# A fused attention and SwiGLU block on one core: the last of the seven products of two output phases is split into seven once more, with its operand sums on VectorE

## The chip, the core and the metric

The kernel runs on one core of a Trainium2 chip. The metric is the device time of one execution in microseconds (us), as the median of several runs. TensorE (PE) does the matrix products and writes to PSUM, which has eight banks of 128x512 fp32. VectorE (DVE) and ScalarE (ACT) read PSUM and the on-chip SBUF, GpSimd (POOL) does a few small operations, and DMA transfers are issued from the queues of SyncE (SP), ACT and POOL. Each engine works through its own instructions in order and waits on semaphores for the others.

## The reference

A transformer block over 2048 rows of width 1024, modulated by a conditioning vector `c`:

```python
mod = (silu(c) @ w_mod).reshape(1, 6, 1, -1)          # sa, ca, ga, sb, cb, gb
h = layernorm(x) * (1 + ca) + sa
q = (h @ wq) as 32 heads of 128                       # keys, values: the last 512 rows of each cache, 4 heads
o = softmax(q k^T * 128**-0.5) v
x = x + ga * (o @ wo)                                 # wo: 4096 x 1024
h = layernorm(x) * (1 + cb) + sb
out = x + gb * ((silu(h @ w_gate) * (h @ w_up)) @ w_down)   # w_gate, w_up: 1024 x 3584, w_down: 3584 x 1024
```

All inputs are bfloat16, and the output is bfloat16.

## The kernel before

The rows are worked in two halves (`sc` 0 and 1) of 1024 rows, first through attention, each half followed by its output phase (`o_phase(sc)`, the product with `wo`), and then through the feed-forward part, each half a run of `gate_up` steps followed by its down phase (the product with `w_down`, called with `f_out` and `f_hook`). In time the order is: attention and output phase of half 0, of half 1, then gate/up and down of half 0, of half 1.

Most large products are not multiplied block by block. A product of 2x2 blocks is written as seven block products in place of eight, of sums and differences of the blocks (the Strassen-Winograd form). For the two output products `seven_products` (L1030) does this. Its left operand is held in four blocks `X[0]` to `X[3]`, each `nk` slices of 128x512 (`nk` is 16 for `wo`, 14 for `w_down`); its right operands are the weights, of which four combined versions were formed earlier by VectorE and written to DRAM (`wo_sum`, `wd_sum`). The products run in the order `ORDER = (1, 2, 6, 5, 3, 7, 4)`, which the text counts as steps 0 to 6. A step has four parts, `j` = 0 to 3, one for each 128 rows, and one part is `nk` matmuls of 128x128 by 128x512 into one bank. PSUM banks hold running totals from one step to the next: `AB[j]` and `BB_[j]` are the two sets of four.

Between the steps VectorE makes the sums of the left operand in place (L1041), ScalarE copies a bank to SBUF (`snap`, L832), and VectorE finishes an output tile in `residual` (L1107) with up to three operations: add of bank and copy (L1117), product with the gate row (L1118), add of `x_res` (L1119). In step 6 one product per part is the whole sum for an output tile, so `residual` takes two operations there, L1112 and L1119. A `hook(idx, j)` after each part runs other work beside the phase: weight loads of a coming step on the ACT queue (`load`), the layer normalisation of the next rows (`ln_pair`, whose modulations are L443), the four sums of the next left operand (`h_sums`, L838 to L850, 128x2048 each), and the sums of the coming gate and up weights (`w_sums` by `ws`, L901).

The order on each engine is the order in which the program emits it; a tracker (`T.op`) adds the semaphore waits that the buffers demand. After an output or down phase comes `gate_up(q, None)` (L1552), which begins with product 1 of the gate weights into bank `ga`, product 2 into `gb_`, a copy of `gb_` on ScalarE, and VectorE's sum `g_sum` (L830) of `ga` and the copy. Then products 1 and 2 of the up weights follow into `ua` and `ub`, a copy and `u_sum` (L830), and then product 6 into `ga` again and later into `ua` again. So product 6 waits until `g_sum` has read `ga`, and until `u_sum` has read `ua`. The gate/up weights come by `take_w(q)` on the SP queue, into three slots in turn.

Memory is one arena with fixed offsets; where two tiles share a place, the later one waits for the users of the earlier.

Of the kernel before, what the change touches and what calls it, by code (L numbers as in the profile page):

```python
# [4 lines left out]
AF = mybir.ActivationFunctionType  # L5
BF16 = mybir.dt.bfloat16
F16 = mybir.dt.float16
# [124 lines left out]
def bass_adaLN_cond__sliding_block_cached__swiglu_ffn__prompt_kernel(  # L132
# [126 lines left out]
    with nc.Block() as block:  # L259

        @block.gpsimd
        def _(g):
# [764 lines left out]

            ORDER = (1, 2, 6, 5, 3, 7, 4)

            def seven_products(nk, X, XBf, offs, s1, ver, AB, BB_, out, sj, own_s1, hook, early=(0,) * 4, halves=False):  # L1030
# [48 lines left out]
                for j in range(TPC):  # L1079
                    prod(3, j, BB_[j], True)  # L1080
                    snap(*sj[j], BB_[j])
                    inplace(3, j, 2, [(jc(X[2], j), jc(X[3], j), jc(X[0], j), [S[2][j]] + XBf[3])])
                    hook(3, j)
                for j in range(TPC):
                    prod(4, j, BB_[j], False)
                    out(0, j, 1, AB[j], BB_[j], None)
                    hook(4, j)
                for j in range(TPC):
                    prod(5, j, AB[j], False)
                    out(1, j, 1, AB[j], None, sj[j])  # L1090
                    hook(5, j)
                for j in range(TPC):
                    if halves and j == TPC - 1:
                        lo, hi = slice(0, CH // 2), slice(CH // 2, CH)
                        T.op(ACT, lambda: A.activation(sj[j][0][:, lo], bank(AB[j])[:, lo], AF.Copy), writes=[PB[AB[j]], sj[j][1]])
                        prod(6, j, BB_[j], True, c=lo)
                        out(1, j, 0, BB_[j], None, sj[j], lo)
                        prod(6, j, AB[j], False, c=hi)
                        out(1, j, 0, AB[j], None, None, hi)
                    else:  # L1100
                        prod(6, j, AB[j], False)
                        out(1, j, 0, AB[j], None, None)
                    hook(6, j)
                for n, blk in ((2, 0), (4, 1), (3, 2)):
                    arena.regs.append((offs[blk], offs[blk] + nk * KB, S[n]))

            def residual(t, c0, row, a_bk, b_bk, sj, ring, dst, db, c=slice(0, CH)):  # L1107
                tm, tb = ring
                tm = tm[:, c]
                rw = rowb[row][:, c0:c0 + CH][:, c]  # L1110
                if b_bk is None and sj is None:
                    T.op(DVE, lambda: V.tensor_tensor(tm, bank(a_bk)[:, c], rw, MULT), reads=[B_row[row]], writes=[PB[a_bk], tb])  # L1112
                else:
                    if b_bk is not None:
                        snap(tm, tb, b_bk)
                        sj = (tm, tb)
                    T.op(DVE, lambda: V.tensor_tensor(tm, bank(a_bk)[:, c], sj[0][:, c], ADD), reads=[sj[1]], writes=[PB[a_bk], tb])  # L1117
# [19 lines left out]
            def loader(sc, raw, sums, nk, kind, places):  # L1137
                pair = raw.rearrange("(p h q) n -> h q p n", h=2, q=P)
                src = {1: pair[0][:, :, 0:CH], 2: pair[1][:, :, 0:CH], 3: pair[1][:, :, CH:D]}
                for n, i in ((5, 1), (6, 2), (4, 3), (7, 0)):  # L1140
                    src[n] = sums[:, :, i, :].rearrange("p q n -> q p n")
                got = {}

                def load(idx, which=None):
                    n = ORDER[idx]
                    dt = BF16 if n < 4 else F16
                    k0 = 0
                    got.setdefault(idx, [])
                    for q, (off, m) in enumerate(places[idx]):
                        if which is not None and q not in which:  # L1150
                            k0 += m
                            continue
                        b_ = _Buf("%sv%d_%d_%d" % (kind, sc, idx, q))
                        ap = arena.at(off, [m, CH], dt, [b_])
                        T.op(Q_ver[q][idx % 3], lambda: A.dma_start(ap, src[n][:, k0:k0 + m, :]),
                             reads=[B_uw[(kind, p)] for p in range(k0, k0 + m)] if n > 3 else [], writes=[b_])
                        got[idx] += [(ap[:, k, :], b_) for k in range(m)]
                        k0 += m

                return load, lambda idx, k: got[idx][k]  # L1160

            def attention(sc, lo, pre, tick):
                hi = (sc + 1) * NI
# [170 lines left out]
            attend(0, 1, pre0, tick0)  # L1334

            def o_out(sc, sj, rings):
                def out(tt, j, half, a_bk, b_bk, s):
                    t = (2 * sc + tt) * TPC + j
                    ring = rings(tt, j, half)
                    residual(t, half * CH, 0, a_bk, b_bk, s, ring, x_res[:, t, half * CH:(half + 1) * CH], B_x[t])  # L1340
                return out

            def o_phase(sc, hook):
# [208 lines left out]
            def gate_up(q, pq, fill=None):  # L1552
# [16 lines left out]
                    snap(*sn[1], xb)  # L1569
                if a:  # L1570
                    g_sum(q, 0, ga, sn[0])
                    if q % FP == 1:
                        ws(2)
                if b:
# [50 lines left out]
                        ws(2)  # L1625

            def f_out(sc):
                def out(tt, j, half, a_bk, b_bk, s, c=slice(0, CH)):
# [4 lines left out]
                    residual(t, c0, 1, a_bk, b_bk, s, tms[i % 2], y_b[:, i, c], B_y[i], c)  # L1633
                    T.op((Q_out + Q_fin)[i], lambda: SP.dma_start(of[t * P:(t + 1) * P, c0:c0 + CH][:, c], y_b[:, i, c]), reads=[B_y[i]])
                return out

            for sc in range(2):
# [7 lines left out]
                for r in range(FP + 1):  # L1645
# [70 lines left out]
```

The softmax here doesn't subtract the row's maximum and nothing guards it: scores larger than these inputs give would overflow.

## Time and profile before

| | |
|---|---|
| median of 4 runs | 1152.6 us (1151.49 to 1152.9) |
| the profiled execution's own time | 1152.76 us |
| its span, first to last instruction | 1151.0 us |
| PE busy | 1143.5 us, 99% of the span |
| DVE busy | 822.5 us, 71% |
| ACT busy | 525.9 us, 46% |
| granted TensorE clock | 1.0 |
| step 6 of the output phase of half 1 | 625.91 to 639.72 us |
| step 6 of the down phase of half 0 | 881.55 to 893.63 us |

How the profile is read: a group row gives line, engine, operation, the tiles it writes and reads, shapes and count, then busy time, the mean duration of one in ns, and the idle time of the engine just before them with what ended it. A timeline row gives start, duration, engine, line and operation, and in square brackets the idle time before it and what ended that. A row by windows gives, for a stretch, its length, the busy time of each engine with the number of instructions touched, the granted clock and the DMA share. Matmuls are pipelined: a 128x512 matmul is shown with some 379 ns from start to end, while the next starts 216 ns after it.

### The profile page before, as it was taken

What the parts mean: (1) busy time and instruction counts of PE and PEld (TensorE: products, weight loads), DVE (VectorE), ACT (ScalarE), POOL (GpSimd) and SP (SyncE); (2) the same over time, 40 slices, a digit from 0 to 9 for tenths busy, and PEclk for the clock granted to TensorE, in tenths of its full rate; (3) what the DMA queues carried; (4) which work ended last, traced back from release to release, by engine and by line L of the source; (5) the groups of instructions that cost most, each with busy time, mean ns of one, the idle gap of its engine ahead of it and who ended that gap; (6) DMA issues with size and microseconds to landing.
All of it is one profiled execution on the core that took longest, in us unless ns stands there. A gap on an engine that the chain in (4) does not pass through costs nothing.

```text
span 1151.0 us, 18014 instructions
## 1 busy us (share of the span) xinstructions
PE 1143.5 (99%) x6991; PEld 584.4 (51%) x6991; DVE 822.5 (71%) x1644; ACT 525.9 (46%) x719; POOL 50.2 (4%) x107
## 2 busy tenths in 40 slices
PE   8999999999999999999999999999999999999999
PEld 5566565554446666566444444444444444444444
DVE  5768779857667777776757789877658777776536
ACT  4757777721127777777010354544110445444110
POOL 1100102100000000001000000000000000000000
DMA  9889999988617998946864423323783433233343
GB/s 317 148 186 225 226 214 218 216 204 202 201 41 179 205 213 188 211 105 156 192 199 128 111 73 87 97 74 106 209 224 121 119 87 97 74 106 131 129 156 110
DMA packets 300373, 180.83 MB, mean 157 GB/s; under 512 B 140928, under 2 KB 289152, under 8 KB 300288
## 3 DMA queue, kind: packets, MB, share of 16 engines
q1 hardware_dynamic: 241632, 108.90, 42.2%
q10 hardware_dynamic: 54336, 55.05, 15.1%
q0 software_dynamic: 4320, 15.73, 4.6%
q8 instruction: 55, 0.90, 0.4%
q14 instruction: 30, 0.25, 0.1%
HBM read 126.75 MB, written 19.93 MB: 127 GB/s over the span
## 4 chain that ended last, share of the span: by engine, by line
PE 97%; DMA 1%; DVE 1%; SPq 0%; ACT 0%; issue 0%; POOLq 0%; DVEq 0%
PE ps L269 97%; DMA arena<-in_A_wq_dram 1%; DMA arena<-in_A_wo_dram 1%; DVE arena L830 0%; ACT arena L800 0%; SPq L337 0%; SPq L306 0%; DVE arena L847 0%; DVE arena L951 0%; DVE arena L901 0%; PE ps L273 0%; DVE st L424 0%; DVE arena L822 0%; DVE tmp L1112 0%; DVE arena L1119 0%
## 5 line engine op out<-in xcount | busy, mean ns | idle before, releaser
L269 PE MATMUL ps<-arena 128*128 128x512 f16 (+2 forms) x6778 | 1138.6, 331 | 4.6 <-POOL arena L416 2.0
L269 PEld LDWEIGHTS ps<-arena 128*128 128x128 bf16 (+1 forms) x6778 | 577.2, 98 | 559.5 <-DVE arena L830 5.8
L800 ACT ACTIVATE arena<-ps 128x1024 bf16<-128x1024 f32 x256 | 261.7, 1022 | 47.0 <-PE ps L269 35.3
L833 ACT ACTIVATE tmp<-ps 128x512 f32<-128x512 f32 x167 | 99.7, 597 | 293.0 <-PE ps L269 282.2
L901 DVE TENSOR_TENSOR arena<-arena 128x512 f16<-128x512 bf16 x328 | 133.5, 420 | 3.0
L830 DVE TENSOR_TENSOR arena<-ps,tmp 128x512 bf16<-128x512 f32 (+1 forms) x134 | 91.9, 686 | 52.1 <-PE ps L269 34.7
L833 ACT ACTIVATE nsc<-ps 128x512 f32<-128x512 f32 x84 | 50.1, 597 | 93.3 <-PE ps L269 90.9
L822 DVE TENSOR_TENSOR arena<-ps,rl 128x512 f16<-128x512 f32 x128 | 88.5, 691 | 4.9 <-DVE rl L819 0.5
L830 DVE TENSOR_TENSOR arena<-ps,nsc 128x512 f16<-128x512 f32 x84 | 57.3, 687 | 40.3 <-PE ps L269 30.0
L819 DVE RECIPROCAL rl<-ps 128x4 f32<-128x4 f32 x128 | 23.2, 181 | 74.6 <-PE ps L269 73.5
L1117 DVE TENSOR_TENSOR tmp<-ps,tmp 128x512 f32<-128x512 f32 x32 | 22.1, 690 | 63.4 <-ACT tmp L833 60.8
L1532 ACT ACTIVATE arena<-arena 128x512 f16<-128x512 f16 x84 | 49.8, 624 | 32.8 <-DVE arena L830 32.8
L1041 DVE TENSOR_TENSOR arena<-arena 128x2048 f16<-128x2048 f16 (+3 forms) x56 | 55.6, 1012 | 9.8 <-PE ps L269 9.2
L833 ACT ACTIVATE arena<-ps 128x512 f32<-128x512 f32 x16 | 9.6, 597 | 91.8 <-PE ps L269 91.8
L951 DVE TENSOR_TENSOR arena<-arena 128x512 f16<-128x512 bf16 x120 | 47.9, 420 | 2.2 <-DMA arena<-in_A_wo_dram 1.2
L424 DVE BATCH_NORM_STATS2 st<-x_res 128x6 f32<-128x512 bf16 x58 | 39.6, 682 | 3.6 <-DMA x_res<-in_A_x_dram 3.4
L602 DVE SCALAR_TENSOR_TENSOR arena<-arena 128x1024 bf16<-128x1024 bf16 x32 | 38.9, 1217 | 0.0
L1547 DVE TENSOR_TENSOR arena<-arena 128x512 f16<-128x512 f16 x84 | 35.0, 417 | 0.3
L1118 DVE TENSOR_TENSOR tmp<-tmp,rowb 128x512 f32<-128x512 f32 (+1 forms) x49 | 33.6, 686 | 1.8
L438 DVE TENSOR_SCALAR nsc<-x_res,mv,rstd 128x1024 f16<-128x1024 bf16 (+1 forms) x30 | 16.2, 539 | 13.5 <-DMA arena<-nsc 13.5
L1119 DVE TENSOR_TENSOR arena<-tmp,x_res 128x512 bf16<-128x512 f32 (+1 forms) x33 | 22.3, 676 | 1.1
L830 DVE TENSOR_TENSOR arena<-ps,rowb 128x512 f16<-128x512 f32 x28 | 19.3, 689 | 3.8 <-ACT rowb L833 3.3
(80 smaller groups left out, 295.0 us busy)
## 6 DMA issues: line engine op xcount, KB each, us to landing
arena<-in_A_wq_dram SPq DMA_DIRECT2D x30, 512.0 KB, 5.2
arena<-wo_sum ACTq DMA_DIRECT2D x7, 2048.0 KB, 8.6
arena<-in_B_w_gate_dram SPq DMA_DIRECT2D x28, 512.0 KB, 3.8
arena<-in_B_w_up_dram SPq DMA_DIRECT2D x28, 512.0 KB, 5.1
arena<-wd_sum ACTq DMA_DIRECT2D x8, 1792.0 KB, 8.1
arena<-in_B_w_down_dram ACTq DMA_DIRECT2D x6, 1792.0 KB, 7.2
arena<-in_A_wo_dram POOLq DMA_DIRECT2D x16, 512.0 KB, 5.9
wo_sum<-arena SPq DMA_DIRECT2D x16, 512.0 KB, 4.5
```

The lines of the kernel that those rows point to most:

```text
L269: T.op(PE, lambda: TE.matmul(out_ap, lhsT, rhs, start=start, stop=stop, skip_group_check=skip), reads=reads, writes=[bank_buf])
L424: T.op(DVE, lambda: V.bn_stats(st_[sl][:, hf * 6:hf * 6 + 6], x_res[:, t, hf * 512:hf * 512 + 512]), reads=[B_x[t]], writes=[B_st[sl]])
L602: T.op(DVE, lambda: V.scalar_tensor_tensor(mt[n % 2], mt[n % 2], 1.0, sc_row, op0=ALU.mult, op1=ALU.mult, accum_out=mcol[:, n:n + 1]), rea ...
L800: T.op(ACT, lambda: A.activation(ex_s[es][:, 2 * kp:2 * kp + 2, :], banks2(SCB + 2 * kp), AF.Exp, scale=att_scale), writes=[PB[SCB + 2 * k ...
L822: T.op(DVE, lambda: V.tensor_tensor(o_s[os_].rearrange("p (a b) d -> p a b d", a=2), psap(PVB * 512, [[512, 2], [130, 2], [1, P]]), rlb, A ...
L830: T.op(DVE, lambda: V.tensor_tensor(out, bank(ba), other, ADD), reads=[ob2], writes=[PB[ba], ob])
L833: T.op(ACT, lambda: A.activation(dst, bank(bk), AF.Copy), writes=[PB[bk], db])
L901: T.op(st, lambda: eng.tensor_tensor(o, a, b, op), reads=rd, writes=[wr])
L951: T.op(DVE, lambda: V.tensor_tensor(o, a, b, SUB), reads=rd, writes=[wr])
L1041: T.op(DVE, lambda: V.tensor_tensor(o, a, b, SUB), reads=rd, writes=[sb])
L1532: T.op(ACT, lambda: A.activation(o, s_, AF.Silu), reads=[sb], writes=[ob])
L1547: T.op(DVE, lambda: V.tensor_tensor(gu[blk][:, p, :], o, s_, MULT), reads=[sb, ob], writes=[B_gu[blk][p]])
```

## The change

Step 6 of two of the four phases, `o_phase(1)` and the down phase of half 0, is no longer four parts of `nk` matmuls 128x512. A class `_Deep` splits this one product again into seven products of halves: `h = nk / 2` slices by `Q = 256` columns, for two groups `g` of rows. `left` makes four sums of the left block `X[3]` after step 3 into the place of the no longer used `X[0]`; `right` makes four sums of the weights of step 6, two within step 5 and two after the first two small products, one of them in place. `run` orders the fourteen small products, and `keep` (ScalarE, 128x256) and `plus` (VectorE, 128x256) carry partial sums from bank to SBUF. The output tiles of this step then need the three operations of `residual` and not two. The second and third of the very last tile are put in `late_out` and emitted inside the next `gate_up`, after its `g_sum`; in the down phase its store goes with them.

Other work changes place in these two phases: `h_sums` goes from step 6 to step 4 (in the down phase its first two operations to the end of step 3), the modulations of `ln_pair` are drained ahead of it, `w_sums` of the down phase goes from step 6 to step 0, the weights of step 6 of the down phase are loaded after part 1 of step 4 (not part 3) into another place and in three transfers, the weights of step 5 in `o_phase(1)` have another place, and the tiles of `o_phase(1)` use `sj[j]` as scratch.

```diff
+late_out = []
...
+class _Deep:
...
+    def left(self, off, free):
+        h, x, Q = self.h, self.x, CH // 2
+        self.b_s = [_Buf("dS%d" % n) for n in range(4)]
+        s = self.s = arena.at(off, [4, h, Q], F16, self.b_s)
+        for b_ in self.b_s:
+            for f in free:
+                b_.absorb(f)
+        a11, a12, a21, a22 = x[:, 0:h, 0:Q], x[:, h:, 0:Q], x[:, 0:h, Q:], x[:, h:, Q:]
+        for (n, a, b, op, rd) in ((0, a21, a22, ADD, []), (1, s[:, 0], a11, SUB, [0]), (3, a12, s[:, 1], SUB, [1]), (2, a11, a21, SUB, [])):
+            T.op(DVE, lambda: V.tensor_tensor(s[:, n], a, b, op), reads=self.xb + [self.b_s[m] for m in rd], writes=[self.b_s[n]])
+            yield
+    def right(self, off, free):
+        h, Q = self.h, CH // 2
+        self.b_t = [_Buf("dT%d" % n) for n in range(3)]
+        self.b_5 = [_Buf("d5%d" % n) for n in range(2)]
+        t = self.t = arena.at(off, [3, h, Q], F16, self.b_t)
+        self.p5 = arena.at(off + 3 * h * Q * 2, [2, Q], F32, self.b_5)
+        for b_ in self.b_t + self.b_5:
+            for f in free:
+                b_.absorb(f)
...
+        for step in (0, 1, 3, 2):
+            for (m0, m1, ((lo, lb, lof), (hi, hb, hof))) in self.segs:
+                o = [t[:, n, m0:m1, :] for n in range(3)]
+                b11, b12, b21, b22 = lo[:, :, 0:Q], lo[:, :, Q:], hi[:, :, 0:Q], hi[:, :, Q:]
+                if step == 3:
+                    b3 = _Buf("dT3")
+                    b3.absorb(lb)
+                    arena.regs.append((lof, lof + (m1 - m0) * KB, [b3]))
+                    self.b_3.append(b3)
+                    T.op(DVE, lambda: V.tensor_tensor(b12, b22, b12, SUB), reads=[hb, lb], writes=[b3])
+                else:
+                    a, b, rd = ((b12, b11, [lb]), (b22, o[0], [hb, self.b_t[0]]), (b21, o[1], [hb, self.b_t[1]]))[step]
+                    T.op(DVE, lambda: V.tensor_tensor(o[step], a, b, SUB), reads=rd, writes=[self.b_t[step]])
+            yield
...
+    def prod(self, n, g, bk, c0, start):
+        h, Q = self.h, CH // 2
+        for m in range(h):
+            sn, i, ((lo, lb, _), (hi, hb, _)) = self.seg(m)
...
+            mm(bank(bk)[:, c0:c0 + Q], la, ra, start and m == 0, m == h - 1, [lb_, rb], PB[bk], skip=True)
...
+    def run(self, AB, BB_, out, sj, hook, sums):
+        Q = CH // 2
+        L, R = slice(0, Q), slice(Q, CH)
+        def keep(dst, db, bk):
+            T.op(ACT, lambda: A.activation(dst, bank(bk)[:, 0:Q], AF.Copy), writes=[PB[bk], db])
+        def plus(dst, db, a, ab, b, bb):
+            T.op(DVE, lambda: V.tensor_tensor(dst, a, b, ADD), reads=[ab, bb], writes=[db])
+        def first(g):
+            self.prod(1, g, BB_[g], 0, True)
+            keep(sj[g][0][:, L], sj[g][1], BB_[g])
+            self.prod(2, g, AB[g], 0, False)
+        def middle(g):
+            lo, lb = sj[g]
+            self.prod(6, g, BB_[g], 0, False)
+            keep(lo[:, R], lb, BB_[g])
+            self.prod(5, g, BB_[2 + g], 0, True)
+            keep(self.p5[:, g, :], self.b_5[g], BB_[2 + g])
+            plus(lo[:, R], lb, lo[:, R], lb, self.p5[:, g, :], self.b_5[g])
+            self.prod(3, g, AB[g], Q, False)
+            out(1, g, 0, AB[g], None, sj[g])
+            hook(6, 2 * g)
+        def last(g, later=None):
+            hi, hb = sj[2 + g]
+            self.prod(7, g, BB_[g], 0, False)
+            keep(hi[:, L], hb, BB_[g])
+            plus(hi[:, R], hb, hi[:, L], hb, self.p5[:, g, :], self.b_5[g])
+            self.prod(4, g, AB[2 + g], 0, False)
+            out(1, 2 + g, 0, AB[2 + g], None, sj[2 + g], later=later)
+            hook(6, 2 * g + 1)
+        first(0)
+        for _ in sums:
+            pass
+        middle(0)
+        first(1)
+        last(0)
+        middle(1)
+        last(1, late_out)
+def seven_products(nk, X, XBf, offs, s1, ver, AB, BB_, out, sj, own_s1, hook, early=(0,) * 4, halves=False, deep=False):
...
         snap(*sj[j], BB_[j])
         inplace(3, j, 2, [(jc(X[2], j), jc(X[3], j), jc(X[0], j), [S[2][j]] + XBf[3])])
         hook(3, j)
+    if deep:
+        dp = _Deep(nk, X[3], XBf[3], ver.runs.setdefault(6, []))
+        for _ in dp.left(offs[0], S[2] + XBf[0]):
+            run_bg(2)
+        hook(3, TPC)
     for j in range(TPC):
         prod(4, j, BB_[j], False)
         out(0, j, 1, AB[j], BB_[j], None)
         hook(4, j)
+    if deep:
+        right = dp.right(offs[1], S[4] + XBf[1])
     for j in range(TPC):
         prod(5, j, AB[j], False)
+        if deep and j in (2, 3):
+            next(right)
         out(1, j, 1, AB[j], None, sj[j])
         hook(5, j)
-    for j in range(TPC):
+    if deep:
+        dp.run(AB, BB_, out, sj, hook, right)
+    for j in range(0 if deep else TPC):
...
-def residual(t, c0, row, a_bk, b_bk, sj, ring, dst, db, c=slice(0, CH)):
+def residual(t, c0, row, a_bk, b_bk, sj, ring, dst, db, c=slice(0, CH), later=None):
...
+        if later is not None:
+            later.append(lambda: T.op(DVE, lambda: V.tensor_tensor(tm, tm, rw, MULT), reads=[B_row[row]], writes=[tb]))
+            later.append(lambda: T.op(DVE, lambda: V.tensor_tensor(dst, tm, x_res[:, t, c0:c0 + CH][:, c], ADD), reads=[tb, B_x[t]], writes=[db]))
+            return
...
-    places = [[(OFF_WQ, 7), (OFF_WQ + 7 * KB, 7), (131 * KB, 2)], [(133 * KB, 12), (OFF_E, 4)]] + [[(o, HP)] for o in (OFF_WQ, OFF_E, OFF_WQ, OFF_N)] + [two]
+    places = [[(OFF_WQ, 7), (OFF_WQ + 7 * KB, 7), (131 * KB, 2)], [(133 * KB, 12), (OFF_E, 4)]] + [[(o, HP)] for o in (OFF_WQ, OFF_E, OFF_WQ, 136 * KB if sc else OFF_N)] + [two]
...
-            return sj[1 + j % 2]
+            return sj[j] if sc == 1 else sj[1 + j % 2]
...
-    seven_products(HP, oT, B_oT, OFF_OT, n1, ver, AB_O, BB_O, o_out(sc, sj, rings), sj, True, hk, (14, 14, 0, 0))
+    seven_products(HP, oT, B_oT, OFF_OT, n1, ver, AB_O, BB_O, o_out(sc, sj, rings), sj, True, hk, (14, 14, 0, 0), deep=sc == 1)
...
-    if idx == 4 and j == TPC - 1:
-        take_w(0)
-    if idx == 5 and j == TPC - 1:
-        while bg:
-            run_bg(1)
-        hs[0] = h_sums()
+    if idx == 4:
+        if j == 0:
+            while bg:
+                run_bg(1)
+            hs[0] = h_sums()
         next(hs[0])
+        if j == TPC - 1:
+            take_w(0)
     if idx == 6:
-        if j < 3:
-            next(hs[0])
         if j == 0:
...
+        while late_out:
+            late_out.pop(0)()
...
+        def store():
+            T.op((Q_out + Q_fin)[i], lambda: SP.dma_start(of[t * P:(t + 1) * P, c0:c0 + CH][:, c], y_b[:, i, c]), reads=[B_y[i]])
+        if later is None:
+            store()
+        else:
+            later.append(store)
     return out
...
-            load, ver = loader(sc, B_w_down, wd_sum, FP, "d", [[(o, FP)] for o in [d0, d1] * 3 + [d0]])
+            load, ver = loader(sc, B_w_down, wd_sum, FP, "d", [[(o, FP)] for o in [d0, d1] * 3] + [[(64 * KB, 4), (152 * KB, 3), (155 * KB, 7)] if sc == 0 else [(d0, FP)]])
...
-        if j == TPC - 1 and idx < 5:
+        if j == TPC - 1 and idx < (4 if sc == 0 else 5):
             load(idx + 2)
+        if sc == 0 and (idx, j) == (4, 1):
+            load(6)
         run_bg(1)
-        if sc == 0 and idx == 6:
+        if sc == 0 and idx == 0:
             if j == 0:
-                while bg:
-                    run_bg(1)
-                hs[0] = h_sums()
                 wsum[0] = w_sums(FP)
+            ws(1)
+        if (sc, idx) == (0, 3) and j == TPC:
+            while bg:
+                run_bg(1)
+            hs[0] = h_sums()
             next(hs[0])
-            ws(1)
-    seven_products(FP, gu, B_gu, OFF_GU, m1, ver, (0, 1, 2, 3), (4, 5, 6, 7), f_out(sc), sj, False, f_hook, (10, 0, 0, 0), sc == 1)
+            next(hs[0])
+        if sc == 0 and idx == 4 and j < 2:
+            next(hs[0])
+    seven_products(FP, gu, B_gu, OFF_GU, m1, ver, (0, 1, 2, 3), (4, 5, 6, 7), f_out(sc), sj, False, f_hook, (10, 0, 0, 0), sc == 1, sc == 0)
```

Everything else, the other two phases included, is as before.

More of the change, by code (lines that the diff above doesn't have):

```diff
@@ L1028, in _, with __init__, seg @@
             ORDER = (1, 2, 6, 5, 3, 7, 4)
-            def seven_products(nk, X, XBf, offs, s1, ver, AB, BB_, out, sj, own_s1, hook, early=(0,) * 4, halves=False):
+            late_out = []
+            class _Deep:
+                def __init__(self, nk, x, xb, runs):
+                    self.nk, self.h, self.x, self.xb, self.runs = nk, nk // 2, x, xb, runs
+                def left(self, off, free):
[18 more added lines that the diff above has]
+                            b_.absorb(f)
+                    cuts = sorted({c % h for r in self.runs for c in r[0:2]} | {0, h})
+                    self.segs = []
+                    for m0, m1 in zip(cuts, cuts[1:]):
+                        at = []
+                        for k in (m0, h + m0):
+                            (k0, k1, o, ap, b_), = [r for r in self.runs if r[0] <= k < r[1]]
+                            at.append((ap[:, k - k0:k - k0 + m1 - m0, :], b_, o + (k - k0) * KB))
+                        self.segs.append((m0, m1, at))
+                    self.b_3 = []
+                    for step in (0, 1, 3, 2):
[12 more added lines that the diff above has]
+                        yield
+                def seg(self, m):
+                    for n, (m0, m1, at) in enumerate(self.segs):
+                        if m0 <= m < m1:
+                            return n, m - m0, at
+                def prod(self, n, g, bk, c0, start):
+                    h, Q = self.h, CH // 2
+                    for m in range(h):
+                        sn, i, ((lo, lb, _), (hi, hb, _)) = self.seg(m)
+                        gs = slice(g * P, (g + 1) * P)
+                        hs_ = slice(Q + g * P, Q + (g + 1) * P)
+                        l = {1: lambda: (self.x[:, m, gs], self.xb[m]), 2: lambda: (self.x[:, h + m, gs], self.xb[h + m]),
+                             4: lambda: (self.x[:, h + m, hs_], self.xb[h + m])}
+                        la, lb_ = l[n]() if n in l else [(self.s[:, q, m, gs], self.b_s[q]) for q in ({5: 0, 6: 1, 7: 2, 3: 3}[n],)][0]
+                        if n in (5, 6, 4):
+                            q = {5: 0, 6: 1, 4: 2}[n]
+                            ra, rb = self.t[:, q, m, :], self.b_t[q]
+                        else:
+                            ra, rb = {1: (lo[:, i, 0:Q], lb), 2: (hi[:, i, 0:Q], hb), 3: (hi[:, i, Q:], hb),
+                                      7: (lo[:, i, Q:], self.b_3[sn] if n == 7 else None)}[n]
+                        mm(bank(bk)[:, c0:c0 + Q], la, ra, start and m == 0, m == h - 1, [lb_, rb], PB[bk], skip=True)
[36 more added lines that the diff above has]
+                    last(1, late_out)
@@ L1141, in loader @@
                     src[n] = sums[:, :, i, :].rearrange("p q n -> q p n")
-                got = {}
+                got, runs = {}, {}
                 def load(idx, which=None):
@@ L1157, in load, with ver @@
                         got[idx] += [(ap[:, k, :], b_) for k in range(m)]
+                        runs.setdefault(idx, []).append((k0, k0 + m, off, ap, b_))
                         k0 += m
-                return load, lambda idx, k: got[idx][k]
+                def ver(idx, k):
+                    return got[idx][k]
+                ver.runs = runs
+                return load, ver
             def attention(sc, lo, pre, tick):
@@ L1336, in o_out, with out @@
             def o_out(sc, sj, rings):
-                def out(tt, j, half, a_bk, b_bk, s):
+                def out(tt, j, half, a_bk, b_bk, s, later=None):
                     t = (2 * sc + tt) * TPC + j
                     ring = rings(tt, j, half)
-                    residual(t, half * CH, 0, a_bk, b_bk, s, ring, x_res[:, t, half * CH:(half + 1) * CH], B_x[t])
+                    residual(t, half * CH, 0, a_bk, b_bk, s, ring, x_res[:, t, half * CH:(half + 1) * CH], B_x[t], later=later)
                 return out
@@ L1627, in f_out, with out @@
             def f_out(sc):
-                def out(tt, j, half, a_bk, b_bk, s, c=slice(0, CH)):
+                def out(tt, j, half, a_bk, b_bk, s, c=slice(0, CH), later=None):
                     t = (2 * sc + tt) * TPC + j
@@ L1632, in out @@
                     cnt["y"] += 1
-                    residual(t, c0, 1, a_bk, b_bk, s, tms[i % 2], y_b[:, i, c], B_y[i], c)
-                    T.op((Q_out + Q_fin)[i], lambda: SP.dma_start(of[t * P:(t + 1) * P, c0:c0 + CH][:, c], y_b[:, i, c]), reads=[B_y[i]])
+                    residual(t, c0, 1, a_bk, b_bk, s, tms[i % 2], y_b[:, i, c], B_y[i], c, later)
+                    def store():
+                        T.op((Q_out + Q_fin)[i], lambda: SP.dma_start(of[t * P:(t + 1) * P, c0:c0 + CH][:, c], y_b[:, i, c]), reads=[B_y[i]])
+                    if later is None:
+                        store()
+                    else:
+                        later.append(store)
                 return out
```

## The prediction, made before the changed kernel was run

> **What bounds the kernel now.** I read the page's busy time and last chain first: TensorE is busy nearly the whole span.
>
> ```profile
> PE 1143.5 (99%) x6991; PEld 584.4 (51%) x6991; DVE 822.5 (71%) x1644; ACT 525.9 (46%) x719; POOL 50.2 (4%) x107
> ...
> PE 97%; DMA 1%; DVE 1%; SPq 0%; ACT 0%; issue 0%; POOLq 0%; DVEq 0%
> ```
>
> So only matmul time and waits of TensorE move the end. Next, busy time by windows: step 6 of the output phase of half 1, step 6 of the down phase of half 0, and the 3.7 us behind each.
>
> ```profile
> 625.91:639.72 13.81, 13.81 (x65) 6.27 (x64) 11.77 (x16) 0.00 (x0) 0.00 (x0) 1.00 0.00 0
> 881.55:893.63 12.08, 12.08 (x58) 5.48 (x57) 10.57 (x15) 0.00 (x0) 0.00 (x0) 1.00 0.16 56
> 639.70:643.40 3.70, 3.70 (x19) 1.67 (x18) 2.41 (x4) 0.99 (x2) 0.00 (x0) 1.00 0.64 185
> 893.60:897.30 3.70, 3.64 (x17) 1.47 (x15) 3.53 (x6) 0.60 (x1) 0.00 (x0) 1.00 0.15 46
> ```
>
> The columns are length, PE, weight loads, DVE, ACT, POOL, clock, DMA. Step 6 is 64 matmuls in 13.81 us and 56 in 12.08: 215.8 ns each, with no gap, at clock 1.00; ScalarE is idle, and VectorE has 2 us and 1.5 us left. After the down phase TensorE starts two matmuls fewer in the same 3.70 us than after the output phase: a wait. The timeline there shows why (start, duration; idle before, releaser):
>
> ```profile
> 642.28 0.69 DVE L830 TENSOR_TENSOR arena<-ps,nsc 128x512 f16<-128x512 f32 x1 [0.60 <-ACT nsc L833]
> 644.15 0.69 DVE L830 TENSOR_TENSOR arena<-ps,nsc 128x512 f16<-128x512 f32 x1 [1.18 <-ACT nsc L833]
> ...
> 896.30 0.42 DVE L901 TENSOR_TENSOR arena<-arena 128x512 f16<-128x512 f16 x1
> 896.63 0.68 DVE L830 TENSOR_TENSOR arena<-ps,nsc 128x512 f16<-128x512 f32 x1
> 897.37 1.41 PEld L269 LDWEIGHTS ps<-arena 128*128 128x128 f16 x8 [0.62 <-DVE arena L830]
> ```
>
> Count from the phase's end E (639.72, 893.63). Product 6 into `ga` is due after four products of 4 x 0.2158, at E+3.45, and into `ua` at E+5.18. g_sum began at E+2.56 in one (limited by ScalarE's copy) and at E+3.00 in the other (VectorE late). u_sum follows 1.87 later through silu and a copy, takes 0.69, and so ends at E+5.12: 0.06 before it is due. In the other it is 0.44 late, and that is the wait (0.29 + 0.14, by the matmul starts). **Every us that VectorE is later than E+2.6 with g_sum costs TensorE a us.**
>
> **The change, part by part.**
>
> *Matmuls.* 64 of 512 columns become 7 x 8 x 2 = 112 of 256, and 56 become 7 x 7 x 2 = 98. The cadence at 256 columns:
>
> ```profile
> 13.83 0.82 PE L269 MATMUL ps<-arena 128*128 128x256 f16 x6
> ...
> L269 PE MATMUL ps<-arena 128*128 128x256 f16 x52 | 6.5, 273 | 0.9 <-DMA arena<-in_A_wq_dram 0.9
> ```
>
> (0.82 - 0.273) / 5 = 109.3 ns. So 13.81 becomes 112 x 0.1093 = 12.24 (-1.57) and 12.08 becomes 98 x 0.1093 = 10.71 (-1.37): **-2.94**, all on TensorE. Two rules of the Trainium skill speak against this. "TensorE: Matmul & The Clock Gate", section Back-to-back issue gap, gives for a sustained stream of weight load and matmul 81 ns at 128 columns and 131 at 512, some 98 at 256 between them: 210 x 98 - 120 x 131 = +4.9 us. But this trace is such a stream and shows 215.8, not 131; I take the rows. "TensorEngine Tiling (Array Packing)", Instruction Overhead, has some 60 cycles more for each matmul; at the 2.4 GHz that the first page states that is 25 ns for 90 more matmuls, 2.25 us, leaving -0.7. Rows: twice 109.3 is only 2.8 ns above 215.8. The weight load (98 ns by its group) still fits into 109.
>
> *VectorE sums.* The 256-column sums of 8 slices are 128x2048, of 7 slices 128x1792. Nearest rows are the in-place sums, strided f16 too:
>
> ```profile
> L1041 DVE TENSOR_TENSOR arena<-arena 128x2048 f16<-128x2048 f16 x24 | 29.0, 1222 | 0.3
> L1041 DVE TENSOR_TENSOR arena<-arena 128x1792 f16<-128x1792 f16 x16 | 16.6, 1085 | 0.0
> L1041 DVE TENSOR_TENSOR arena<-arena 128x1280 f16<-128x1280 f16 x8 | 6.6, 825 | 0.3
> L1041 DVE TENSOR_TENSOR arena<-arena 128x512 f16<-128x512 f16 x8 | 3.4, 424 | 9.2 <-PE ps L269 9.2
> ```
>
> In a row they follow each other about 0.09 sooner: 1.13 and 1.00. In the down phase the weights' sums are cut (128x1024 and 128x768, between rows: 0.69 and 0.56, 1.07 together). Bounds: 1.0, and, at the fp32 slope (0.69 and 0.42 for 512 and 256 elements: 1.05 ns each), 2.30 for 2048. I take the f16 rows; the upper end is a rival.
>
> *Left sums*, 4.5 and 4.0 us, go into idle time, with the eight pulled-forward modulations (2.6 to 2.9):
>
> ```profile
> 602.57 0.69 DVE L1117 TENSOR_TENSOR tmp<-ps,tmp 128x512 f32<-128x512 f32 x1 [11.77 <-ACT tmp L833]
> 861.22 0.69 DVE L1117 TENSOR_TENSOR tmp<-ps,tmp 128x512 f32<-128x512 f32 x1 [7.79 <-ACT tmp L833]
> ```
>
> In the output phase, free. In the down phase two next-operand sums (2.3) come as well: 853.4 + 4.0 + 2.6 + 2.3 = 862.3, 1.1 late for the output at 861.22. Each part of step 4 is 3.02 us on TensorE; the outputs take 2.06, two more sums 1.13 each. VectorE catches up at 872.7, when step 5's first output is due. No bank is needed before 869.5, so it is free. In the output phase step 4 takes 2.06 + 1.13 = 3.19 of 3.45 per part.
>
> *Weights of step 6* must now be in SBUF for VectorE in step 5. Output phase: issued at 601.9, landed at 612.4, first read near 621.3. Down phase: issued near 863.6 in place of 869.7, three transfers, behind one still moving until 866.2; at some 8 us for 1792 KB (by the page's issues) they land at 872 to 874, for a read at 877.8. Nothing waits; if they were late, the VectorE operations queued behind would be, and then g_sum. The down phase's moved gate/up sums (4 x 0.42 in step 0) wait for a load that landed at 814.25, and fit into idle gaps of 1.1 to 1.7 us.
>
> *The tail, output phase.* Small product boundaries are 0.874 apart from 625.91, E' = 638.15. VectorE starts 0.2 after a boundary; a 256-column copy is 0.39 (a row at 1136.82). Outputs of parts 0 and 1 of step 5 end at 618.2 and 621.3; sum to 622.4; output 624.7; sum 625.8; output 628.2; two sums 630.4. Product 6 wants the second sum at 627.66, product 7 the third at 632.03, product 4 the last at 632.91: all early. A keep takes 0.2 + 0.39 + 0.04 = 0.63 before the same bank is wanted, 0.874 later (0.765 in the down phase): hidden, by 0.24 and 0.13. Then per tile plus 0.46, three operations 2.06, L901 0.35: tiles end at 633.3, 636.4 and 639.3, and the last needs only plus, one add and L901: 640.77 = E'+2.62. g_sum is not later than before (+2.56) by more than 0.06. The two late operations (0.73 + 0.61) stand between g_sum and u_sum; u_sum would be free 1.95 after g_sum's start, not 1.87: 0.08. Stall 0.1.
>
> *The tail, down phase.* Boundaries 0.765 apart from 881.55, E' = 892.26. From 878.83 VectorE never waits but once: output 880.9, sums 882.0, output 884.0, sums 886.2, then tiles at 888.7, 891.2, 893.7 (no L901 here), plus and add 894.8 = E'+2.54; the copy allows E'+2.56. `ub`'s bank is read until 894.9, due at 894.85. Stall 0.1 to 0.2, where there is 0.43 now: -0.3.
>
> *SP's queue.* In the output phase the third pair of weight loads waits for VectorE's last add, E'+2.3 for E+1.7 now; its first use is 22 products later, E+19. In the down phase the first pair leaves near E'+1.6 for E+2.15 now. The late store goes behind both pairs; its tile is rewritten some 8 us later. POOL gets nothing.
>
> **Sum.** -1.57 - 1.37 + 0.1 - 0.3 = -3.1 on the span: 1147.9. The profiled execution was 1152.76 (1.76 around its span), so 1149.6; the median lies 0.16 lower, so **1149.5**.
>
> **The rivals.** *VectorE's tail is late.* In both tails it hardly rests, and their lengths are my sums of some 25 operations. 0.1 us each on eight operations is 0.8 on each tail: 1151.1; 1.5 on each gives all back, 1152.5. Also the short keeps: 0.2 more on four costs 0.3 to 0.4. For: no slack stands in the sum. Against: every duration has a near row.
> *The matmuls don't shrink so far*: the 60-cycle rule, 1151.7. Against it the cadence row.
> *Slower: the strided sums run at the fp32 rate*, +1.08 on each 2048 sum. The four weights' sums then add 4.3 to the output phase's tail and 3.8 to the down phase's, whose left sums add another 2 after catching up: +10 - 3 = +7, 1159.6. It decides from about +0.6 us per sum, where the tails lose 5.4. The L1041 rows speak against it. A load landing 9 us late would do the same at one place.
>
> **How the numbers follow.** 0.2% is 2.3 us, what a measurement of this kernel can tell from no change: below 1150.3 is faster, above 1154.9 slower. Likeliest case 0.60 (1148.9 to 1150.3); tail late 0.25 (1150.3 to 1153); matmul overhead 0.04; slower 0.11. A small part of the second (0.01) still ends below 1150.3: faster 0.61, same 0.24 + 0.04 = 0.28, slower 0.11. The range 1148.8 to 1152.8 leaves out the slower case and the end of the second.
>
> **What would show it.** Right: step 6 in some 12.3 and 10.8 us; g_sum within E'+2.7; the new sums near 1.2 us, the cut ones 0.7 and 0.6; no wait of TensorE on ScalarE's keeps. Wrong: g_sum later than E'+3.5, weight sums idle on a DMA, small products over 109 ns apart, or a new wait in the steps before.

## The result and the profile after

The changed kernel takes 1149.83 us (median of 39 runs, 1148.81 to 1152.58) against 1152.45 us (median of 59 runs, 1151.43 to 1153.88). The ratio is 0.9979, 95% interval 0.9974 to 0.9983: 2.6 us less, with 2.0 to 3.0 inside the interval. The profiled span is 1147.2 us, where that of before is 1151.0. A run's time is longer than its span: by 1.8 us for the kernel before (median of 60 runs taken beside the experiments), and by 2.2 for the changed kernel. So some 2.9 us of span (medians of 1150.5 and 1147.6) became 2.6 us of time. o_only and f_only below, with one phase changed each, still have 1.8, and no run shows where these 0.4 us come from.

The two profiled spans differ by 3.74 us (1150.96 and 1147.22 before rounding). Of these, 0.88 lie ahead of the change: the output phase's step 6 starts at 625.03 in one profile and at 625.91 in the other, though what comes before it runs the same matmuls. From the start of that step to the end, the two traces differ by 2.86 us (525.05 and 522.19). Busy time by windows of the changed kernel, again with length, PE, weight loads, DVE, ACT, POOL, clock and DMA, shows the two steps and the 3.7 us behind each:

```profile
625.03:637.26 12.23, 12.23 (x114) 10.96 (x113) 11.51 (x19) 3.07 (x8) 0.00 (x0) 1.00 0.01 2
879.13:889.83 10.70, 10.70 (x100) 9.56 (x99) 10.32 (x19) 3.07 (x8) 0.00 (x0) 1.00 0.11 38
637.26:640.96 3.70, 3.70 (x20) 1.69 (x18) 3.63 (x8) 1.02 (x2) 0.00 (x0) 1.00 0.93 258
889.83:893.53 3.70, 3.35 (x17) 1.38 (x15) 3.60 (x7) 0.63 (x2) 0.00 (x0) 1.00 0.22 73
```

The steps take 12.23 us (13.81 before) and 10.70 (12.08 before), without a gap between matmuls: 109.2 ns each. The weight loads now fill 89 to 90% of the step and still hide. VectorE fills 94 and 96%. Behind the output phase there is hardly a wait; behind the down phase TensorE is idle for 0.35 us of the 3.70, and the timeline there says for whom:

```profile
891.72 0.42 DVE L1113 TENSOR_TENSOR arena<-arena 128x256 f32<-128x256 f32 x1
891.75 0.60 ACT L833 ACTIVATE nsc<-ps 128x512 f32<-128x512 f32 x1 [2.11 <-PE ps L269]
892.17 0.69 DVE L1247 TENSOR_TENSOR tmp<-ps,arena 128x512 f32<-128x512 f32 x1
892.78 0.68 DVE L830 TENSOR_TENSOR arena<-ps,nsc 128x512 f16<-128x512 f32 x1
892.92 2.27 PEld L269 LDWEIGHTS ps<-arena 128*128 128x128 bf16 x12 [0.84 <-DVE tmp L1247]
```

With the phase's end E' at 889.83, the product into `ub` is due at E'+2.59 = 892.42. That bank is still read by the last tile's add (L1247), which ends at 892.86, and the matmul starts at 892.92: 0.50 late. g_sum (L830) starts at E'+2.95; it would have made product 6, the one after it, late by some 0.25 us (an estimate from the 0.29 of the kernel before, where g_sum began at E+3.00), had TensorE not been late already. Both stand in the same VectorE queue, and the cause is that this queue is late.

### The profile page after: what moved, and what is told of

Read it like the earlier page. It is cut to its first block, busy times and chain, and to the rows that moved or that the text cites. A ratio compares the mean times of both kernels' runs of the same rounds, so it can differ in the third digit from the quotient of the medians.

```text
span 1147.2 us, 18268 instructions
## 1 busy us (share of the span) xinstructions
PE 1140.4 (99%) x7081; PEld 593.4 (52%) x7081; DVE 847.8 (74%) x1680; ACT 531.9 (46%) x735; POOL 50.6 (4%) x107
## 4 chain that ended last, share of the span: by engine, by line
PE 98%; DMA 1%; DVE 0%; SPq 0%; ACT 0%; issue 0%
PE ps L269 98%; DMA arena<-in_A_wq_dram 1%; ACT arena L800 0%; DVE arena L830 0%; SPq L337 0%; SPq L306 0%; DVE arena L847 0%; PE ps L273 0%; DVE tmp L1247 0%; DVE tmp L1242 0%; DVE arena L1253 0%; DVE arena L1113 0%; DVE arena L901 0%
## 5 line engine op out<-in xcount | busy, mean ns | idle before, releaser
L269 PE MATMUL ps<-arena 128*128 128x512 f16 (+3 forms) x6868 | 1135.5, 328 | 3.9 <-POOL arena L416 2.0
L269 PEld LDWEIGHTS ps<-arena 128*128 128x128 bf16 (+1 forms) x6868 | 586.1, 98 | 547.0 <-DVE arena L830 4.3
L830 DVE TENSOR_TENSOR arena<-ps,tmp 128x512 bf16<-128x512 f32 (+1 forms) x134 | 91.9, 686 | 52.1 <-PE ps L269 34.7
L830 DVE TENSOR_TENSOR arena<-ps,nsc 128x512 f16<-128x512 f32 x84 | 57.2, 686 | 37.4 <-PE ps L269 30.0
L1247 DVE TENSOR_TENSOR tmp<-ps,tmp 128x512 f32<-128x512 f32 x32 | 22.1, 689 | 46.2 <-ACT tmp L833 43.6
L1110 ACT ACTIVATE arena<-ps 128x256 f32<-128x256 f32 x16 | 6.1, 384 | 40.6 <-PE ps L269 40.6
```

The costliest lines, as they stand in the source:

```text
L269: T.op(PE, lambda: TE.matmul(out_ap, lhsT, rhs, start=start, stop=stop, skip_group_check=skip), reads=reads, writes=[bank_buf])
L830: T.op(DVE, lambda: V.tensor_tensor(out, bank(ba), other, ADD), reads=[ob2], writes=[PB[ba], ob])
```

## The experiments

A single time scatters by 2 to 4 us, and the traces show where most of that lies: before the output phase there is a wait of 0.25 us that every trace has, and it ends anywhere from 538.9 to 540.8 us. So the table counts from there to the end of the span, beside the timed ratio to the kernel before. Each experiment was timed next to the kernel before, whose median was then 1152.1 to 1152.4 us; their medians are of 10 or 11 runs (down_sums_in_step6: four). The stretch is read from one trace of each. "Wait" is what TensorE loses behind the phase, summed from matmul starts farther apart than their size asks for. For down_sums_in_step6 this includes slower matmuls.

| kernel | step 6 output, down (us) | wait behind each (us) | rest of span (us) | less than before | median (us) | ratio (95%) |
|---|---|---|---|---|---|---|
| before | 13.81, 12.08 | 0.00, 0.43 | 611.09 | | 1152.45 | |
| changed | 12.23, 10.70 | 0.05, 0.51 | 608.23 | 2.86 | 1149.83 | 0.9979 (0.9974 to 0.9983) |
| o_only | 12.23, 12.08 | 0.05, 0.43 | 609.56 | 1.53 | 1151.76 | 0.9993 (0.9984 to 1.0002) |
| f_only | 13.81, 10.69 | 0.00, 0.50 | 609.76 | 1.33 | 1151.06 | 0.9988 (0.9979 to 0.9997) |
| moves_only | 13.81, 12.08 | 0.00, 0.00 | 610.65 | 0.44 | 1152.08 | 0.9999 (0.9990 to 1.0008) |
| down_sums_in_step6 | 12.22, 10.69 | 0.05, 7.0 | 614.72 | -3.63 | 1156.43 | 1.0039 (1.0025 to 1.0053) |
| whole_weights | 12.23, 10.69 | 0.05, 0.05 | 607.78 | 3.31 | 1149.39 | 0.9975 (0.9966 to 0.9984) |
| down_tail_less | 12.22, 10.70 | 0.05, 0.05 | 607.77 | 3.32 | one run | |
| down_tail_more | 12.22, 10.70 | 0.05, 1.42 | 609.14 | 1.95 | one run | |
| two_tiles_late | 12.23, 10.70 | 0.00, 0.00 | 607.66 | 3.43 | 1149.55 | 0.9975 (0.9966 to 0.9984) |
| piece_buffers | 12.22, 10.70 | 0.05, 0.06 | 607.79 | 3.30 | 1149.38 | 0.9974 (0.9964 to 0.9984) |

**One phase alone.** In o_only the down phase is that of the kernel before, in f_only the output phase is:

```diff
# o_only
-[[(o, FP)] for o in [d0, d1] * 3] + [[(64 * KB, 4), (152 * KB, 3), (155 * KB, 7)] if sc == 0 else [(d0, FP)]]
+[[(o, FP)] for o in [d0, d1] * 3 + [d0]]
-seven_products(FP, gu, ..., (10, 0, 0, 0), sc == 1, sc == 0)      # and f_hook as before
+seven_products(FP, gu, ..., (10, 0, 0, 0), sc == 1)
...
# f_only
-seven_products(HP, oT, ..., (14, 14, 0, 0), deep=sc == 1)         # and o_hook1, places, rings as before
+seven_products(HP, oT, ..., (14, 14, 0, 0))
```

> Only the output phase of half 1 is split (its moved sums with it); the down phase is as before. My theory, matmul time alone moves the end: step 6 of the output phase takes 12.2 us in place of 13.8, a wait of 0.05 behind it, the 0.43 us wait behind the down phase stays: 1.5 us faster than before. Rival, the gain comes from the down phase and its removed wait: 0.5 or less here.

> Only the down phase of half 0 is split, with its moved sums; the output phase is as before. My theory: step 6 of the down phase 10.7 us in place of 12.1, wait behind it about 0.5 us where before has 0.43: 1.3 us faster than before. Rival, the two phases interact (VectorE or the transfers of one help the other): its gain and that of the split output phase alone do not add up to the 2.6 us of both.

In the traces they save 1.53 and 1.33 us, and 1.53 + 1.33 = 2.86 is what both save together. Each phase's gain is its own, and the rivals fall. The timed medians (0.6 and 1.3 us less, 1.8 together for 2.6) don't contradict this, but the interval of o_only runs from 1.8 us faster to 0.2 slower; the times alone would not have settled it.

**The moves without the split.**

```diff
-seven_products(HP, oT, ..., (14, 14, 0, 0), deep=sc == 1)
+seven_products(HP, oT, ..., (14, 14, 0, 0))
...
+                hook(3, TPC)               # the down phase's moved work still runs here
                 if deep:
                     dp = _Deep(...)
...
-seven_products(FP, gu, ..., (10, 0, 0, 0), sc == 1, sc == 0)
+seven_products(FP, gu, ..., (10, 0, 0, 0), sc == 1)
```

> No product is split; step 6 has its four parts of 512 columns again, but the next operand's sums, the gate/up weight sums, the loads and the scratch places stay where the change puts them. My theory: the wait behind the down phase came from VectorE's sums in step 6, so with these moved it goes from 0.43 us to under 0.1, and the kernel is 0.4 us faster than before; so the split itself brings 2.3 to 2.5 of the 2.6 us. Rival, the moved work only changes place: as before, with the wait of 0.43 still there; or slower than before by a new wait in step 4 or 5.

The timeline of this kernel behind its down phase (E' at 892.64) shows VectorE idle before g_sum, which starts as soon as the copy has ended, and TensorE's weight load for product 6 released at E'+3.30. The last line is that weight load behind the output phase of the kernel before, at E+3.30:

```profile
894.56 0.60 ACT L833 ACTIVATE nsc<-ps 128x512 f32<-128x512 f32 x1 [25.30 <-PE ps L269]
895.19 0.69 DVE L830 TENSOR_TENSOR arena<-ps,nsc 128x512 f16<-128x512 f32 x1 [0.94 <-PE ps L269]
895.94 1.55 PEld L269 LDWEIGHTS ps<-arena 128*128 128x128 f16 x8 [0.18 <-DVE arena L830]
...
643.02 1.55 PEld L269 LDWEIGHTS ps<-arena 128*128 128x128 f16 x8 [0.18 <-DVE arena L830]
```

The wait of 0.43 is gone, and with it 0.44 us of the rest of the span; no new wait appears. The timed ratio, 0.9999 with 0.9 us to both sides, can't show a gain of this size. So, by the traces, the moves alone gain 0.4 us, but the split takes the freed VectorE time back: in the changed kernel the wait stands at 0.51 again.

**The moves undone under the split.**

```diff
-if sc == 0 and idx == 0: ... wsum[0] = w_sums(FP); ws(1)
-if (sc, idx) == (0, 3) and j == TPC: ... hs[0] = h_sums(); next(hs[0]); next(hs[0])
-if sc == 0 and idx == 4 and j < 2: next(hs[0])
+if sc == 0 and idx == 6:
+    if j == 0: ... hs[0] = h_sums(); wsum[0] = w_sums(FP)
+    next(hs[0])
+    ws(1)
```

> As the changed kernel, but the next operand's four sums and the four gate/up weight sums of the down phase go back into step 6. My theory, each us that VectorE is late with g_sum costs a us: some 5.9 us more work stand in the tail (4 x 1.13 and 4 x 0.34), the wait behind the down phase grows from 0.5 to some 6 us, and the kernel is 3 us slower than before (1155 to 1156). Rival, these sums are hidden in step 6 as they were in the kernel before: 2.6 us faster than before, as the changed kernel.

It is 4.0 us slower than before, 6.6 slower than the changed kernel. g_sum starts at E'+8.82 where the changed kernel has E'+2.95: 5.87 us later for the 5.9 us of work. But the rest of the span grows by 6.5 us. TensorE is not only idle afterwards; it runs slower, as the windows of this kernel show (E' is 890.39):

```profile
890.40:893.90 3.50, 1.02 (x6) 0.29 (x4) 3.40 (x7) 0.00 (x0) 0.00 (x0) 1.00 0.11 37
893.90:895.90 2.00, 2.00 (x8) 0.80 (x8) 1.97 (x3) 0.60 (x1) 0.00 (x0) 0.77 0.00 0
897.88:901.90 4.02, 3.84 (x9) 1.18 (x10) 3.95 (x7) 1.11 (x2) 0.00 (x0) 0.51 1.13 307
902.00:906.00 4.00, 4.00 (x20) 1.80 (x19) 1.79 (x5) 1.19 (x2) 0.00 (x0) 1.00 0.84 213
```

After a first wait of 2.6 us the granted clock (the third column from the end) falls, and behind a second of 1.8 us it is 0.51: nine matmuls stand in 4.02 us, 0.6 us of it a third wait, where twenty stand in 4.00 us later on. Product 6 into `ga` starts at 899.95, where it was due at E'+3.45 = 893.84. These 6.1 us are VectorE's lateness; the other 0.9 of the 7.0 us are slow matmuls behind it. The split is a gain only because the eight operations of the down phase had been moved out of step 6: left there, they cost 6.5 us, more than twice what it saves.

**VectorE's tail, one operation less and two more.** Down_tail_less leaves out the gate product of one output tile, so that its output tile isn't scaled; down_tail_more repeats an addition.

```diff
# down_tail_less, in residual
+drop = row == 1 and t == TPC + 1 and c0 == 0
-T.op(DVE, lambda: V.tensor_tensor(tm, tm, rw, MULT), ...)
+if not drop:
+    T.op(DVE, lambda: V.tensor_tensor(tm, tm, rw, MULT), ...)
...
# down_tail_more, in last(g)
 plus(hi[:, R], hb, hi[:, L], hb, self.p5[:, g, :], self.b_5[g])
+if self.nk == FP and g == 1:
+    for _ in range(2):
+        plus(hi[:, R], hb, hi[:, L], hb, self.p5[:, g, :], self.b_5[g])
```

> As the changed kernel, but one output tile of step 6 of the down phase (the third) leaves out its product with the gate row, a VectorE operation of 0.73 us in the tail. My theory: g_sum comes as early as ScalarE's copy allows, E'+2.56, and the wait falls from 0.51 to about 0.1. Rival, the wait is due to something other than VectorE's queue (the bank of the last tile, the late store, a weight load): it stays at 0.5.

> As the changed kernel, but the last small addition of 256 columns in the down phase is done three times in place of once, the same result each time: 2 x 0.46 = 0.92 us more on VectorE in the tail. My theory: g_sum 0.92 later, the wait grows from 0.51 to 1.4 us, one for one. Rival, VectorE has slack before g_sum, or the wait is another's: it stays near 0.5.

With 0.73 us less, g_sum starts at E'+2.56 and the wait is 0.05. With 0.92 more it starts at E'+3.87, and the wait grows from 0.51 to 1.42, one for one. The timeline of the second, with E' at 890.03:

```profile
891.92 1.34 DVE L1113 TENSOR_TENSOR arena<-arena 128x256 f32<-128x256 f32 x3
893.29 0.69 DVE L1250 TENSOR_TENSOR tmp<-ps,arena 128x512 f32<-128x512 f32 x1
893.90 0.68 DVE L830 TENSOR_TENSOR arena<-ps,nsc 128x512 f16<-128x512 f32 x1
894.04 3.19 PE L269 MATMUL ps<-arena 128*128 128x512 f16 x14 [1.26 <-DVE tmp L1250]
```

So VectorE's queue sets this wait, and it has no slack.

**Why the queue is late: the cut sums.** Three kernels shorten it in different ways. Whole_weights loads step 6's weights in one piece, so that the sums are not cut:

```diff
-[[(o, FP)] for o in [d0, d1] * 3] + [[(64 * KB, 4), (152 * KB, 3), (155 * KB, 7)] if sc == 0 else [(d0, FP)]]
+[[(o, FP)] for o in [d0, d1] * 3] + [[(d0, FP)]]
-if j == TPC - 1 and idx < (4 if sc == 0 else 5):
+if j == TPC - 1 and idx < 5:
     load(idx + 2)
-if sc == 0 and (idx, j) == (4, 1):
-    load(6)
```

> As the changed kernel, but the weights of step 6 of the down phase go in one transfer into the place that step 4 frees, issued after step 4 as in the kernel before, so that each of their four sums is one of 128x1792 and not two. My theory: the cut sums took 4.74 us in place of the 4.28 that I had worked out, and this is the 0.4 us that g_sum is late; whole they take 4 x 1.0 or little more, g_sum comes at E'+2.6, and the wait behind the down phase falls from 0.51 to 0.1. Rival, the transfer lands too late for the first sum (issued near 867.3, 8 us: 875.3, wanted at 875.3), VectorE stands behind it, and the wait stays or grows by what it is late.

```profile
877.18 1.09 DVE L1080 TENSOR_TENSOR arena<-arena 128x1792 f16<-128x1792 f16 x1
...
884.30 1.08 DVE L1080 TENSOR_TENSOR arena<-arena 128x1792 f16<-128x1792 f16 x1
885.30 0.42 DVE L1113 TENSOR_TENSOR arena<-arena 128x256 f32<-128x256 f32 x1
...
894.19 0.69 DVE L830 TENSOR_TENSOR arena<-ps,nsc 128x512 f16<-128x512 f32 x1 [0.21 <-PE ps L269]
```

The four sums take 1.08 to 1.09 us each, 1.00 to the next operation, as the groups' row for 128x1792 said. The load is only just in time: issued at 869.06, it landed at 877.15, and the first sum reads it at 877.18. So the rival was missed by hundredths of a us. Then g_sum starts at E'+2.56 (E' is 891.63), with VectorE idle before it, and the wait is 0.05. The cut sums of the changed kernel, for comparison, in its timeline:

```profile
875.34 1.35 DVE L1080 TENSOR_TENSOR arena<-arena 128x1024 f16<-128x1024 f16 x2
878.66 1.28 DVE L1080 TENSOR_TENSOR arena<-arena 128x1024 f16<-128x1024 f16 x2
881.91 1.15 DVE L1077 TENSOR_TENSOR arena<-arena 128x1024 f16<-128x1024 f16 x2
882.99 1.28 DVE L1080 TENSOR_TENSOR arena<-arena 128x1024 f16<-128x1024 f16 x2
```

Each row is a pair of pieces. The pieces last 0.68 and 0.56, as estimated; but three pairs take 1.28 to 1.35, and one, on L1077, takes 1.15. Only the pieces on L1077 have a buffer each in the tracker. The two pieces of the others share one, so that the second waits on VectorE's own semaphore for the first to end. Piece_buffers gives every piece a buffer of its own and changes nothing else:

```diff
-self.b_t = [_Buf("dT%d" % n) for n in range(3)]
+self.b_t = [[_Buf("dT%d_%d" % (n, m)) for m in range(len(cuts) - 1)] for n in range(3)]
...
-T.op(DVE, lambda: V.tensor_tensor(o[step], a, b, SUB), reads=rd, writes=[self.b_t[step]])
+T.op(DVE, lambda: V.tensor_tensor(o[step], a, b, SUB), reads=rd, writes=[self.b_t[step][sg_]])   # and the reads of b_t by piece too
...
-ra, rb = self.t[:, q, m, :], self.b_t[q]
+ra, rb = self.t[:, q, m, :], self.b_t[q][sn]
```

> As the changed kernel, but the two pieces of each cut weight sum of the down phase carry a dependency of their own, where they share one: the second piece no longer waits on VectorE's semaphore for the first. My theory: three of the four pairs took 1.19 to 1.27 us and the one without that wait 1.08, so this wait is the term that I had left out; without it all four take 1.06 to 1.08, 0.4 us goes from the tail, g_sum comes at E'+2.56 and the wait behind the down phase falls from 0.51 to about 0.1. Rival, a piece of 1024 or 768 elements just takes that long in a row: pairs of 1.2 and a wait of 0.5 as before.

```profile
875.27 1.15 DVE L1080 TENSOR_TENSOR arena<-arena 128x1024 f16<-128x1024 f16 x2
878.40 1.15 DVE L1080 TENSOR_TENSOR arena<-arena 128x1024 f16<-128x1024 f16 x2
881.52 1.15 DVE L1077 TENSOR_TENSOR arena<-arena 128x1024 f16<-128x1024 f16 x2
882.59 1.15 DVE L1080 TENSOR_TENSOR arena<-arena 128x1024 f16<-128x1024 f16 x2
...
892.31 0.69 DVE L830 TENSOR_TENSOR arena<-ps,nsc 128x512 f16<-128x512 f32 x1
```

All four pairs are now 1.15 us, 1.07 to the next operation; g_sum starts at E'+2.56, and the wait falls from 0.51 to 0.06. The rival, that the pieces just take that long, falls.

**Taking work out of the tail.**

```diff
-def middle(g):
+def middle(g, later=None):
-    out(1, g, 0, AB[g], None, sj[g])
+    out(1, g, 0, AB[g], None, sj[g], later=later)
-middle(1)
+middle(1, late_out if self.nk == FP else None)
...
     g_sum(q, 0, ga, sn[0])
-    while late_out:
-        late_out.pop(0)()
...
     u_sum(q, 0, ua, sn[0])
+    while late_out:
+        late_out.pop(0)()
```

> As the changed kernel, but in the down phase the third tile's last two operations and its store are also put off, and in both phases the put-off operations stand behind u_sum and not between g_sum and u_sum. My theory: g_sum at E'+2.56 in the down phase, u_sum 1.87 later, waits of 0.0 to 0.1 behind both phases where the changed kernel has 0.05 and 0.51: 0.45 us faster than the changed kernel, 3.1 to 3.3 faster than before. Rival, the work put off comes back: the copies of the gate_up step behind it wait for the scratch that these operations read, or its VectorE work runs late, and a new wait of 0.3 or more shows within 15 us.

Both waits are gone, and no new one shows up to the end: the rest of the span is 607.66, the shortest, 0.57 below the changed kernel. The last three kernels of this kind (whole_weights, piece_buffers, two_tiles_late) all lie 2.7 to 3.0 us below the kernel before in time. Their intervals reach into that of the changed kernel, so that they beat it by 0.4 to 0.6 us is shown by the traces and not by the times. All three remove the same wait of 0.5 us behind the down phase, so their gains should not add up; no run combines them.

## Why the prediction was right, point by point

- *Matmul time sets the end, -2.94.* Right: step 6 went down by 1.58 and 1.38 us, 109.2 ns per matmul of 256 columns. The row of the trace was right against both rules that the prediction took from the Trainium skill (some 98 ns for 256 columns against 131 for 512; 25 ns more for each matmul): two matmuls of 256 columns take 2.6 ns more than one of 512 (2 x 109.2 against 215.8). o_only and f_only show the two parts to be additive.
- *No wait on the keeps, none on the weights of step 6, none in steps 4 and 5.* Right: no matmul start in step 6 or in steps 4 and 5 is late by more than 0.03 us. In the down phase the three transfers landed by 870.5 and were first read at 875.3.
- *The tail of the output phase.* g_sum at E'+2.56 for a predicted +2.62, u_sum late by the operations put between, a wait of 0.05 for 0.1.
- *The tail of the down phase.* Here a size was off. The predicted g_sum at E'+2.54 came at E'+2.95, the wait was 0.51 for 0.1 to 0.2, and the change from before is +0.08 us and not -0.3. The term mis-sized is "1.07 together" for a cut sum: 4.28 us for four pairs, where the trace has 4.74. The pieces were sized right; left out was that the second waits for the first. With nothing to spare in this queue, 0.4 us of VectorE became 0.4 us of wait. This is the first rival ("VectorE's tail is late"), in one of the two tails and small. The prediction had also weighed the bank of `ub`, and it was on this one, just before `ga`, that TensorE stood first.
- *The sum.* -3.1 was predicted on the span, -2.86 is what the traces have from step 6 on. That 1149.5 and 1149.83 lie so near is in part luck. The saving was 0.24 smaller than predicted, and the time beyond the span is 2.20 us and not the 1.76 that was carried over. Against these 0.7 us stands 0.3: the sum started from a profile with a longer span than most runs have (1151.0, less 0.16, where the median is 1150.5).
- *The slower rival's cause*, sums at the fp32 rate, did not come: 1.22 us for 128x2048. What such a lateness costs, down_sums_in_step6 shows: with VectorE 5.9 us late behind one phase the kernel is slower than before.
- *Open:* why one start of the output phase comes up to 1.9 us after another was not studied. The profiles differ there by waits within the attention part (for one, near 188 us, of 0.0 to 1.2), which no edit here touches.

## What to carry to other kernels

When one engine is busy for 99% of the span, price a change by counting its instructions at their start-to-start distance, and then look for the first two or three things that it waits for behind the changed stretch; here that came within 0.3 us of the traced gain. Splitting work for the bound engine moves load to its helper, so check the helper's queue at the end of the stretch: what can run in an earlier idle stretch, or after the first hand-over, belongs there. Two instructions that write different parts of one tile should not share a dependency: on VectorE the needless wait cost 0.12 us and more for each pair here, and TensorE 0.45 us in all.

## What the runs showed of the hardware that was not expected

- Two VectorE operations that need nothing of each other start 0.60 us apart when the first lasts 0.69 (875.27 and 875.87 in piece_buffers). With a wait on the first one's semaphore between them it is 0.72 us (twice in the changed kernel), and 0.79 in the one pair that waits there for a transfer's semaphore too. So waiting for the own engine costs 0.12 us here.
- Behind a wait of 2.6 us TensorE ran at half speed (down_sums_in_step6). From 1.1 us after the matmuls had begun again, they started 427 ns apart and not 216, at a granted clock of 0.50 between 894.98 and 901.80, with two more waits in between. The waits of 0.5 and 1.4 us behind the same phase in other traces left the clock at 1.00. The Trainium skill, page "TensorE: Matmul & The Clock Gate", section Part 1: The HAM clock gate (the "warmup" mystery), has the clock halved after an idle window of some 3.4 us; here it fell after a shorter wait, in one trace (the mean clock of this kernel's four runs is 0.997 to 0.999).
